# Attention and mixture of experts on one core: the 128-token slots move inside the 512-token windows, and three of them become 64-token slots with stacked halves

## The chip, the cores and the metric

The kernel runs on one core of a Trainium2 chip. The metric is the device time of one execution in microseconds. A measurement of this kernel can tell about 1% from no change.

## The reference

```python
scores = scale * np.matmul(q, k.transpose(0, 1, 3, 2))      # B=8, H=8, S=576, D=64
scores = np.where(masks[None], scores, -1e9)               # local (32 back) or strided (every 32nd)
attn = exp(scores - max); attn = attn / (attn.sum(-1) + 1e-09)
x = np.matmul(attn, v)  ->  [N=4608, D=512]
logits = x @ w_gate                                         # 8 experts
expert_idx = np.argmax(logits, axis=1)
for e in range(E):
    mask = expert_idx == e
    h = np.maximum(x[mask] @ w1[e], 0.0)                    # w1: 512 x 1024
    out[mask] = gate_w[mask, None] * (h @ w2[e])            # w2: 1024 x 512
```

Everything is float32. With the inputs that the reference draws, the eight experts get 591, 497, 610, 490, 661, 437, 657 and 665 tokens.

## The kernel before

The kernel first computes the attention, batch by batch, writes the rows x to DRAM (`xd`) and works out on the chip which token goes to which expert. The experts' work is cut into *jobs*. A **window** (`window`) is one expert's first 512 tokens: four tiles of 128. Experts 0, 2, 4 and 6 have two of their four tiles done early, in small windows (kind "F") beside the second half of the attention, so in the last phase (kind "B") experts 1, 3, 5 and 7 have windows of four tiles and experts 0, 2, 4 and 6 windows of two. What an expert has beyond 512 tokens goes into **slots** (`slot`): eight slots of up to 128 tokens, always all eight; which expert a slot serves is known only on the chip (`sids`, `souts` and `srow`, made by `e_slots1` to `e_slots4` on VectorE). What eight slots can't hold would go into a loop of dynamic slots at the end (`dynamic_slot`).

Every job streams its expert's weights in four chunks of 1 MB (`Chunk`): a DMA on SP's queue into `raw`, then ScalarE rounds it to `whi` (line 407) and VectorE makes the rest `wlo` (line 411), each in two halves of 128x1024. A product of float32 matrices is three TensorE products (high by high, high by low, low by high). Per chunk a slot does: 12 products of 256 columns (lines 602 to 604), a ReLU out of PSUM (`hr`, line 609 or VectorE), two 128x128 transposes (line 616), a split into `shh` (ScalarE) and `shl` (VectorE), and six products of 512 columns (lines 630 to 632). So each chunk of a slot passes from TensorE to ScalarE, back to TensorE, to ScalarE, to VectorE and back. A window's products are lines 530 to 532 and 503 to 505.

The order of the instructions on every engine is fixed when the program is built: a planner (`Line`) keeps a model of engines, buffers and eight PSUM banks, and again and again issues the operation that can start first, or of those near the first the one with the lowest `prio`, a due time. The costs and due times are written by hand. Each engine then runs its list in order on the chip. The jobs of the last phase have these due times, one after the other, each with a span of its own:

```python
jobs = [("w", 0)]
for e in range(1, E - 1):
    jobs += [("w", e), ("s", e - 1)]
jobs += [("s", s) for s in range(E - 2, RSLOT)] + [("w", E - 1)]
```

All weight chunks, of windows and slots, are chained (`chain_cp`): a chunk's rounding on ScalarE comes after that of the chunk that was added before it.

Of the kernel before, what the change touches and what calls it, by code (L numbers as in the profile page):

```python
# [36 lines left out]
RSLOT = 8  # L37
MAXSLOT = 40
# [13 lines left out]
AHEAD = 12000.0  # L52
F_LOAD = 92500.0
# [246 lines left out]
def moe_attn(ctx, tc, lqk, vl, sqk, vs, wg, wcat, blob, out):  # L300
# [50 lines left out]
    spacer = const.tile([128, 1], F32, name="spacer")  # L351

# [30 lines left out]
    chain_cp = [None]  # L383

    class Chunk:


        def __init__(self, prio, span, kind, load, deps=()):
# [11 lines left out]
            for h in range(2):  # L400
# [13 lines left out]
                hi = add(ACT, act_ns(1024), e_hi, [self.ld, chain_cp[0]], get=[self.hl] if h == 0 else [], put=[raw] if h else [],  # L414
                         prio=prio + 0.1 * span * h, kind=kind)
                lo = add(DVE, dve_ns(1024), e_lo, [hi], put=[raw], prio=prio + 0.1 * span * h, kind=kind)
                chain_cp[0] = hi
                self.parts.append((hi, lo))

    def gather_op(tag, pool, idc, rows, prio, kind, deps, cell):  # L420
        g = Slot(tag)

        def e_gather(_):
            cell["xg"] = buf(pool(), [128, XW], F32, "xg", g)
# [6 lines left out]
    def finish_ops(cell, yb, fin_deps, odc, slot_g, slots_y, ytag, ypool, prio, kind):  # L431
# [3 lines left out]
        def e_fin(e):  # L435
            y = buf(ypool(), [128, DM], F32, "y", yo)
            cell["y"] = y
# [5 lines left out]
        f = add(EITHER, eng, e_fin, fin_deps, get=[yo], put=[*slots_y, slot_g], prio=prio, kind=kind)  # L443
# [8 lines left out]
    def window(e, ranks, start, span, kind, deps, odeps, small, rows=N + 1, final=False):  # L452

        nt = len(ranks)

# [13 lines left out]
        for dc in range(4):  # L469
# [11 lines left out]
            def e_sp(e, dc=dc):  # L481
# [3 lines left out]
                     prio=start - AHEAD + 5.0 * dc, kind=kind, ins=2 * nt)  # L485
            h = add(ACT, act_ns(n), e_sp, [tr], put=[v, vn], prio=start - AHEAD + 5.0 * dc + 1, kind=kind)
            lo = add(DVE, dve_ns(n), e_sp, [h], put=[v, vn], prio=start - AHEAD + 5.0 * dc + 1, kind=kind)
# [68 lines left out]
    def slot(s, start, span, deps):  # L556

        kind = "B"

        def at(u):  # L560
            return start + span * u
# [3 lines left out]
        ga, g = gather_op("xg", lambda: moe["xgm"], lambda: sids[:, s:s + 1], N + 1, at(-0.8), kind, deps, cell)  # L565
# [3 lines left out]
        def e_tr(_):  # L569
            K["xh"] = buf(moe["slp"], [128, 4, 128], F32R, "sxh", sx)  # L570
            K["xl"] = buf(moe["slp"], [128, 4, 128], F32R, "sxl", sx)
            K["tb"] = bank(v)
            for dc in range(4):
                nc.tensor.transpose(K["tb"][:, dc * 128:(dc + 1) * 128], cell["xg"][:, dc * 128:(dc + 1) * 128], ident)

        def e_sp(e):
            split_to(K["tb"], K["xh"].rearrange("p c k -> p (c k)"), K["xl"].rearrange("p c k -> p (c k)"), e)

        tr = add(PE, 360, e_tr, [ga], get=[v, vn, sx], put=[g], prio=start - AHEAD, kind=kind, ins=8)
        h = add(ACT, act_ns(512), e_sp, [tr], put=[v, vn], prio=start - AHEAD + 1, kind=kind)  # L580
        lo = add(DVE, dve_ns(512), e_sp, [h], put=[v, vn], prio=start - AHEAD + 1, kind=kind)
# [7 lines left out]

        m2 = None  # L590
        for c in range(NCH):
            ch = Chunk(at(0.2 * c - 0.25), span, kind, lambda raw, c=c: load(c, raw), deps)
# [4 lines left out]
            def e_mm1(_, C=C, ch=ch, hb=hb):  # L597
                C["b"] = bank(hb)
                for dc in range(4):
                    w = slice(dc * CW, (dc + 1) * CW)  # L600
                    b = C["b"][:, 0:CW]
                    nc.tensor.matmul(b, K["xh"][:, dc, :], ch.hi[:, w], start=(dc == 0), stop=False)
                    nc.tensor.matmul(b, K["xh"][:, dc, :], ch.lo[:, w], start=False, stop=False)
                    nc.tensor.matmul(b, K["xl"][:, dc, :], ch.hi[:, w], start=False, stop=(dc == 3))

            def e_relu(e, C=C, hr=hr):
                C["r"] = buf(moe["slp"], [128, CW], F32, "hr", hr)
                if e == ACT:
# [4 lines left out]
            def e_ht(_, C=C, tv=tv):  # L613
                C["tb"] = bank(tv)
                for fl in range(2):
                    nc.tensor.transpose(C["tb"][:, fl * 128:(fl + 1) * 128], C["r"][:, fl * 128:(fl + 1) * 128], ident)

            def e_hs(e, C=C, sh=sh):
                if e == ACT:
                    C["h"] = buf(moe["slp"], [128, CW], F32R, "shh", sh)  # L620
                    C["l"] = buf(moe["slp"], [128, CW], F32R, "shl", sh)
                split_to(C["tb"][:, 0:CW], C["h"], C["l"], e)

            def e_mm2(_, C=C, ch=ch, c=c):
                if c == 0:
                    K["y"] = bank(yslot)
                for fl in range(2):
                    w = slice(1024 + fl * 512, 1024 + fl * 512 + 512)
                    ts = slice(fl * 128, (fl + 1) * 128)
                    nc.tensor.matmul(K["y"], C["h"][:, ts], ch.hi[:, w], start=(c == 0 and fl == 0), stop=False)  # L630
                    nc.tensor.matmul(K["y"], C["h"][:, ts], ch.lo[:, w], start=False, stop=False)
                    nc.tensor.matmul(K["y"], C["l"][:, ts], ch.hi[:, w], start=False, stop=(c == NCH - 1 and fl == 1))

            p = 0.2 * c
            m1 = add(PE, 12 * mm_ns(256), e_mm1, [*ch.parts[0], h, lo], get=[hb, hn], put=[sx], prio=at(p), kind=kind, ins=24)
            r = add(EITHER, both(256), e_relu, [m1], get=[hr], put=[hb, hn], prio=at(p + 0.001), kind=kind)
            ht = add(PE, 150, e_ht, [r], get=[tv, tn], put=[hr], prio=at(p + 0.002), kind=kind, ins=4)
            hh = add(ACT, act_ns(256), e_hs, [ht], get=[sh], put=[tv, tn], prio=at(p + 0.003), kind=kind)
            hl = add(DVE, dve_ns(256), e_hs, [hh], put=[tv, tn], prio=at(p + 0.004), kind=kind)
            m2 = add(PE, 6 * mm_ns(512), e_mm2, [hh, hl, *ch.parts[1]], get=[yslot, yhold] if c == 0 else [], put=[sh, ch.hl],  # L640
                     prio=at(p + 0.29), kind=kind, ins=12)
        return finish_ops(cell, lambda: K["y"], [m2], lambda: souts[:, s:s + 1], g, [yslot, yhold], "yo", lambda: moe["yp"], at(1.0), kind)
# [42 lines left out]
    def e_tiny(_):  # L685
# [529 lines left out]

    def prefix(src, name):
        for sh in (1, 2, 4):
            nx = pool().tile([128, E], F32, name=f"{name}{sh}")
            nc.vector.tensor_copy(out=nx[:, 0:sh], in_=src[:, 0:sh])
            nc.vector.tensor_tensor(out=nx[:, sh:E], in0=src[:, sh:E], in1=src[:, 0:E - sh], op=ALU.add)  # L1220
            src = nx
        return src

    def before(n, cum, weight, name):

        ge = wide(n, E)
        nc.vector.tensor_tensor(out=ge, in0=iota_sb[:, 0:n].unsqueeze(2).broadcast_to([128, n, E]),
                                in1=cum.unsqueeze(1).broadcast_to([128, n, E]), op=ALU.is_ge)
        es = pool().tile([128, n], F32, name=f"{name}_es")
        nc.vector.tensor_reduce(out=es, in_=ge, axis=AX.X, op=ALU.add)  # L1230
        nc.vector.tensor_tensor(out=ge, in0=ge, in1=weight.unsqueeze(1).broadcast_to([128, n, E]), op=ALU.mult)
        us = pool().tile([128, n], F32, name=f"{name}_us")
        nc.vector.tensor_reduce(out=us, in_=ge, axis=AX.X, op=ALU.add)
        nc.vector.tensor_tensor(out=us, in0=iota_sb[:, 0:n], in1=us, op=ALU.subtract)
# [11 lines left out]
    def e_slots1(_):  # L1246
        rem = pool().tile([128, E], F32, name="rem")
        nc.vector.tensor_scalar(out=rem, in0=cnt, scalar1=-float(BASE), scalar2=0.0, op0=ALU.add, op1=ALU.max)
        it128 = pool().tile([128, 32], F32, name="it128")
        nc.vector.tensor_scalar(out=it128, in0=iota_sb[:, 0:32], scalar1=128.0, scalar2=None, op0=ALU.mult)  # L1250
        cmp = wide(E, 32)
        nc.vector.tensor_tensor(out=cmp, in0=rem.unsqueeze(2).broadcast_to([128, E, 32]),
                                in1=it128.unsqueeze(1).broadcast_to([128, E, 32]), op=ALU.is_gt)
        sl["all"] = pool().tile([128, E], F32, name="rte")
        nc.vector.tensor_reduce(out=sl["all"], in_=cmp, axis=AX.X, op=ALU.add)
        sl["near"] = pool().tile([128, E], F32, name="near")
        nc.vector.tensor_scalar(out=sl["near"], in0=sl["all"], scalar1=float(NEAR), scalar2=None, op0=ALU.min)

    def e_slots2(_):
        sl["cum"] = prefix(sl["near"], "cumn")  # L1260

    def e_slots3(_):
        sl["es"], sl["us"] = before(RSLOT, sl["cum"], sl["near"], "st")

    def e_slots4(_):
        es, us = sl["es"], sl["us"]
        key = pool().tile([128, RSLOT], F32, name="skey")
        nc.vector.scalar_tensor_tensor(out=key, in0=us, scalar=float(E), in1=es, op0=ALU.mult, op1=ALU.add)
        no = pool().tile([128, RSLOT], F32, name="sno")
        nc.vector.tensor_scalar(out=no, in0=es, scalar1=float(E), scalar2=1000.0, op0=ALU.is_equal, op1=ALU.mult)  # L1270
        nc.vector.tensor_tensor(out=key, in0=key, in1=no, op=ALU.add)
# [5 lines left out]
        sf = pool().tile([128, RSLOT], F32, name="sf")  # L1277
        nc.vector.tensor_reduce(out=sf, in_=sel, axis=AX.X, op=ALU.add)
        nc.vector.tensor_copy(out=sids, in_=sf)
        out_index(souts, sf)  # L1280
        weight_row(srow, es)

    def e_slots5(_):
        had = sl["had"] = pool().tile([128, E], F32, name="had")
# [258 lines left out]
```

## Time and profile before

| | us |
|---|---|
| median of three runs | 669.93 |
| lowest, highest | 667.33, 671.51 |
| the profiled execution, its own time | 669.38 |
| its span, first to last instruction | 667.5 |

The profile is one execution. Its engines are PE (TensorE products), PEld (TensorE weight loads), DVE (VectorE), ACT (ScalarE), POOL (GpSimd) and SP (the queue of the weight DMAs). Products on PE overlap in a pipeline, so the duration of one is longer than the step from one to the next; the step is read from the starts in the timeline. "x" is a count; "<-" behind an idle time names what ended it.

### The profile page before, as it was taken

Reading aid. Unit: us, or ns where it says so; the run is one execution under the profiler, and the core shown is the slowest. Engines: PE = TensorE matmul, PEld = TensorE weight load, DVE = VectorE, ACT = ScalarE, POOL = GpSimd, SP = SyncE. Lnnn points to the kernel's source line nnn. Section 1 sums busy time; section 2 is a strip of 40 time slices with the busy share of each in tenths; the row PEclk is TensorE's granted clock in tenths of the full one; section 3 lists DMA queues with packets and bytes.
Section 4 is the critical chain, followed back from the end, with each engine's and each line's share of the span. In section 5 each row is a group of like instructions: output and inputs, shape, how many; then the busy total and the mean of one; then the engine's idle time right before and its main releaser. Section 6 shows DMA issues by size and latency. Waiting matters only on the chain. (4 is left out here: it accounts for less than half of the span.)

```text
span 667.5 us, 14798 instructions
## 1 busy us (share of the span) xinstructions
PE 628.3 (94%) x5927; PEld 523.2 (78%) x5928; DVE 410.7 (62%) x808; ACT 383.8 (57%) x736; POOL 180.7 (27%) x263
## 2 busy tenths in 40 slices
PE   4999989999999989999989999989999989998996
PEld 3777766887878778988878988878978878987884
DVE  3979887658776788862428672437672447688410
ACT  3687857575667575552356662366663366688311
POOL 3557545223516043120051220051210051110002
PEclk9999998999999999999999999999999999999999
DMA  8688859865554399653177673268682358596001
GB/s 336 228 294 299 271 183 402 318 227 203 181 193 168 108 395 384 240 178 139 64 251 289 212 291 148 87 229 297 213 324 102 108 200 324 206 314 247 4 0 66
DMA packets 30937, 145.58 MB, mean 218 GB/s; under 512 B 4750, under 2 KB 4878, under 8 KB 20625
## 3 DMA queue, kind: packets, MB, share of 16 engines
q1 hardware_dynamic: 23616, 123.78, 51.0%
q0 software_dynamic: 6432, 20.26, 8.4%
q8 instruction: 48, 0.79, 0.5%
q10 hardware_dynamic: 816, 0.56, 0.3%
q14 instruction: 25, 0.20, 0.1%
HBM read 125.41 MB, written 20.22 MB: 218 GB/s over the span
## 5 line engine op out<-in xcount | busy, mean ns | idle before, releaser
L411 DVE TENSOR_TENSOR wlo<-raw,whi 128x1024 fp32r<-128x1024 f32 x160 | 192.2, 1229 | 70.1 <-ACT whi L407 67.4
L407 ACT CAST whi<-raw 128x1024 fp32r<-128x1024 f32 x160 | 164.7, 1054 | 54.0 <-PE b L505 41.0
L530 PE MATMUL b<-xh,whi 128*128 128x256 f32 (+1 forms) x384 | 125.7, 327 | 0.5 <-issue 0.5
L532 PE MATMUL b<-xh,wlo 128*128 128x256 f32 (+1 forms) x384 | 123.3, 321 | 1.3 <-DVE wlo L411 1.1
L531 PE MATMUL b<-xl,whi 128*128 128x256 f32 (+1 forms) x384 | 122.7, 320 | 0.5 <-DVE xl L375 0.4
L540 ACT ACTIVATE hh<-b 128x256 fp32r<-128x256 f32 (+1 forms) x96 | 43.7, 455 | 122.0 <-PE b L532 118.4
L503 PE MATMUL b<-whi,hh 128*128 128x512 f32 x256 | 103.3, 404 | 2.0 <-ACT whi L407 1.4
L505 PE MATMUL b<-whi,hl 128*128 128x512 f32 x256 | 101.0, 395 | 1.4 <-DVE hl L543 1.4
L543 DVE SCALAR_TENSOR_TENSOR hl<-b,hh 128x256 fp32r<-128x256 f32 (+1 forms) x96 | 48.2, 507 | 86.4 <-ACT hh L540 86.2
L504 PE MATMUL b<-wlo,hh 128*128 128x512 f32 x256 | 100.9, 394 | 0.0
L530 PEld LDWEIGHTS b<-xh,whi 128*128 128x128 f32 x384 | 72.4, 189 | 9.0 <-issue 0.6
L532 PEld LDWEIGHTS b<-xh,wlo 128*128 128x128 f32 x384 | 72.4, 188 | 8.6 <-DVE wlo L411 3.0
L531 PEld LDWEIGHTS b<-xl,whi 128*128 128x128 f32 x384 | 72.5, 189 | 7.8 <-DVE xl L375 0.9
L425 POOL DMA_INDIRECT xg<-xd,ids x24 | 24.8, 1032 | 195.7 <-ACT y L439 163.6
L505 PEld LDWEIGHTS b<-whi,hl 128*128 128x128 f32 x256 | 48.0, 188 | 13.8 <-DVE hl L543 2.9
L503 PEld LDWEIGHTS b<-whi,hh 128*128 128x128 f32 x256 | 48.1, 188 | 10.5 <-ACT whi L407 1.6
L504 PEld LDWEIGHTS b<-wlo,hh 128*128 128x128 f32 x256 | 48.2, 188 | 8.0
L815 DVE TENSOR_REDUCE nm<-b 128x4 f32<-128x384 f32 (+2 forms) x64 | 32.9, 522 | 20.5 <-PE b L795 15.8
L446 POOL DMA_INDIRECT out_dram<-y,oids x24 | 27.8, 1158 | 63.2 <-ACT y L439 58.5
L375 DVE TENSOR_TENSOR xl<-b,xh 128x256 fp32r<-128x256 f32 (+1 forms) x48 | 23.4, 508 | 31.4 <-ACT xh L373 29.4
L848 POOL TENSOR_TENSOR probl<-probl,ri 128x384 f32<-128x384 f32 (+1 forms) x40 | 30.2, 762 | 43.4 <-DVE ri L844 32.3
L320 ACT COPY pT<-b 96x512 f32<-96x512 f32 (+3 forms) x62 | 33.6, 558 | 11.4 <-PE b L857 10.3
(176 smaller groups left out, 1099.7 us busy)
## 6 DMA issues: line engine op xcount, KB each, us to landing
raw<-in_wcat_dram SPq DMA_DIRECT2D x80, 1024.0 KB, 4.9
xd<-xr SPq DMA_DIRECT2D x36, 264.0 KB, 4.2
lqk_sb<-in_lqk_dram SPq DMA_DIRECT2D x16, 592.0 KB, 6.4
sqk_sb<-in_sqk_dram SPq DMA_DIRECT2D x16, 576.0 KB, 6.4
vst<-in_vs_dram SPq DMA_DIRECT2D x8, 704.0 KB, 9.1
vt<-in_vl_dram SPq DMA_DIRECT2D x8, 640.0 KB
xg<-xd,ids POOLq DMA_INDIRECT x24
out_dram<-y,oids POOLq DMA_INDIRECT x24
```

Source lines behind the costliest of these rows:

```text
L320: nc.scalar.copy(out=out, in_=in_)
L407: nc.scalar.copy(out=self.hi[:, sl], in_=self.raw[:, sl])
L411: nc.vector.tensor_tensor(out=self.lo[:, sl], in0=self.raw[:, sl], in1=self.hi[:, sl].bitcast(F32), op=ALU.subtract)
L503: nc.tensor.matmul(Y[t], H["h"][:, ts], ch.hi[:, w], start=(j == 0), stop=False)
L504: nc.tensor.matmul(Y[t], H["h"][:, ts], ch.lo[:, w], start=False, stop=False)
L505: nc.tensor.matmul(Y[t], H["l"][:, ts], ch.hi[:, w], start=False, stop=(j == 7))
L530: nc.tensor.matmul(b, ch.hi[:, w], X["h"][:, dc, :], start=(dc == 0), stop=False)
L531: nc.tensor.matmul(b, ch.hi[:, w], X["l"][:, dc, :], start=False, stop=False)
L532: nc.tensor.matmul(b, ch.lo[:, w], X["h"][:, dc, :], start=False, stop=(dc == 3))
L540: nc.scalar.activation(out=H["h"][:, 0:n], in_=H["b"][:, 0:n], func=AF.Relu)
L543: nc.vector.scalar_tensor_tensor(out=H["l"][:, 0:n], in0=H["b"][:, 0:n], scalar=0.0, in1=H["h"][:, 0:n].bitcast(F32), op0=ALU.max, op1=ALU ...
L815: nc.vector.tensor_reduce(out=nm[:, 0:nb], in_=sb[k][:, 0:w].rearrange("p (n k) -> p n k", k=step)[:, :, 0:win], axis=AX.X, op=ALU.max)
```

## The change

- A window's due times now hold its slots as well: `WITH` lists which slots run inside which expert's window. A window's span grows by 11 us for each full slot and 8 us for each short one, and the slots' due times are spread over it. Windows 1, 3 and 5 (four tiles) hold slots 0; 1 and 6; 2 and 3. Windows 2, 4 and 6 (two tiles) hold slots 5; 7; 4. Windows 0 and 7 hold none.
- The slots' weight chunks are chained among themselves, apart from those of the windows.
- Slots 5, 6 and 7 are short: up to 64 tokens. Their high and low halves lie side by side in one stationary operand, so that two products take the place of three; the two halves of the result lie in partitions 0 to 63 and 64 to 127. After the first layer a float32 product with `twice` (two 64x64 identities, one above the other) transposes and adds them, in place of the transpose; after the second layer ScalarE copies one half and VectorE adds the other, and ScalarE scales the sum.
- `e_slots1` to `e_slots5` sort the extra pieces into those over 64 tokens (slots 0 to 4) and those of up to 64 (slots 5 to 7), with more small VectorE instructions.
- Windows of the last phase have the transposes of their x due 18 us ahead in place of 12.

```diff
+RFULL = 5
+WITH = ((), (0,), (5,), (1, 6), (7,), (2, 3), (4,), ())
+SPLIT = 4000.0
+LATER = 3500.0
+STRETCH = 0.85
+FIRST_AT = 0.05
+AHEAD_W = 18000.0
...
-    chain_cp = [None]
+    chain_cp = {}
...
-                hi = add(ACT, act_ns(1024), e_hi, [self.ld, chain_cp[0]], ...
+                hi = add(ACT, act_ns(1024), e_hi, [self.ld, chain_cp.get(chain)], ...
...
+        def e_other(_):
+            cell["y"] = buf(ypool(), [128, DM], F32, "y", yo)[0:n]
+            nc.scalar.copy(out=cell["y"], in_=yb()[n:2 * n])
+        def e_sum(_):
+            nc.vector.tensor_tensor(out=cell["y"], in0=yb()[0:n], in1=cell["y"], op=ALU.add)
+        if n < 128:
+            f = add(ACT, 560, e_other, fin_deps, get=[yo], prio=prio, kind=kind)
+            f = add(DVE, 650, e_sum, [f], put=slots_y, prio=prio, kind=kind)
+            f = add(ACT, 600, e_fin, [f], put=[slot_g], prio=prio, kind=kind)
...
-    def slot(s, start, span, deps):
+    def slot(s, start, step, deps):
+        short = s >= RFULL
+        n = 64 if short else 128
...
+            if short:
+                K["h"], K["l"] = K["xh"][:, :, 0:n], K["xh"][:, :, n:2 * n]
...
+        def products(out, high, low, ch, w, first, last):
+            nc.tensor.matmul(out, high, ch.hi[:, w], start=first, stop=False)
+            nc.tensor.matmul(out, high, ch.lo[:, w], start=False, stop=short and last)
+            if not short:
+                nc.tensor.matmul(out, low, ch.hi[:, w], start=False, stop=last)
...
-            ch = Chunk(at(0.2 * c - 0.25), span, kind, lambda raw, c=c: load(c, raw), deps)
+            p = start + step * c
+            ch = Chunk(p - SPLIT, 12000.0, kind, lambda raw, c=c: load(c, raw), deps, "s")
...
+                    if short:
+                        nc.tensor.matmul(C["tb"][:, fl * n:(fl + 1) * n], C["r"][:, fl * 128:(fl + 1) * 128], twice, start=True, stop=True)
+                    else:
+                        nc.tensor.transpose(C["tb"][:, fl * n:(fl + 1) * n], C["r"][:, fl * 128:(fl + 1) * 128], ident)
...
+                if e == ACT:
+                    nc.scalar.activation(out=x[:, :, 0:n], in_=t, func=AF.Relu)
+                else:
+                    nc.vector.scalar_tensor_tensor(out=x[:, :, n:2 * n], in0=t, scalar=0.0, in1=x[:, :, 0:n].bitcast(F32),
+                                                   op0=ALU.max, op1=ALU.subtract)
...
+            ht = add(PE, 150, e_ht, [r, doubled], get=[tv, tn], put=[hr], prio=p + 20, kind=kind, ins=4)
...
+    def e_twice(_):
+        nc.gpsimd.tensor_tensor(out=twice, in0=ident[:, 0:64], in1=ident[:, 64:128], op=ALU.add)
...
+        for e in range(E):
+            tr = range(2 if e in EXP else 0, 4)
+            span = 11000.0 * len(tr) + sum(8000.0 if x >= RFULL else 11000.0 for x in WITH[e])
+            for n, x in enumerate(WITH[e]):
+                scattered = slot(x, start + span * (n + FIRST_AT) / len(WITH[e]), span * STRETCH / len(WITH[e]) / NCH, [sized, *allrows])
+            window(e, [(lambda t=t, e=e: ids[:, t, e:e + 1], lambda t=t, e=e: oids[:, t, e:e + 1]) for t in tr],
+                   start, span, "B", [made, *allrows], [mout], False, final=e == E - 1)
+            start += span
```

## Rows read from the trace of the kernel before

**Rows 1.** The page, busy time of each engine over the whole span, and TensorE's clock.

```profile
PE 628.3 (94%) x5927; PEld 523.2 (78%) x5928; DVE 410.7 (62%) x808; ACT 383.8 (57%) x736; POOL 180.7 (27%) x263
PEclk9999998999999999999999999999999999999999
```

**Rows 2.** Busy time by stretch, last phase: stretch, its length, each engine, clock, DMA.

```profile
214.00:338.00 124.00, 119.57 (x784) 101.12 (x783) 76.15 (x165) 62.85 (x103) 22.59 (x32) 1.00 0.57 213
338.00:360.00 22.00, 19.37 (x132) 17.02 (x131) 14.24 (x20) 15.13 (x28) 10.17 (x14) 1.00 0.68 239
...
436.00:460.00 24.00, 21.36 (x141) 18.64 (x140) 15.49 (x21) 15.99 (x28) 10.67 (x15) 1.00 0.67 225
...
536.00:558.00 22.00, 19.36 (x130) 16.97 (x130) 14.52 (x20) 15.13 (x27) 10.17 (x14) 1.00 0.65 228
558.00:600.00 42.00, 42.00 (x281) 37.90 (x280) 29.76 (x37) 29.95 (x49) 3.98 (x6) 1.00 0.81 282
600.00:616.00 16.00, 14.25 (x88) 11.94 (x88) 12.71 (x16) 12.43 (x22) 1.09 (x2) 1.00 0.71 254
```

**Rows 3.** Waits of PE from 338 to 616 us: total, times, longest.

```profile
PE b L630 <- ACT shh L373: 6.8, 6, 1.5
PE b L616 <- ACT hr L609: 1.6, 2, 0.8
```

**Rows 4.** Groups by line and shape, one line of each kind of product.

```profile
L602 PE MATMUL b<-whi,sxh 128*128 128x256 f32 x128 | 37.7, 295 | 0.0
...
L631 PE MATMUL b<-wlo,shh 128*128 128x512 f32 x64 | 25.3, 396 | 0.0
...
L999 PE MATMUL b<-xT,wg_sb 128*32 128x384 f32 x96 | 10.6, 495 | 0.0
```

**Rows 5.** Timeline of PE: start, duration. Products of 256 and 512 columns, and transposes.

```profile
358.23 0.28 PE L530 MATMUL b<-xh,whi 128*128 128x256 f32 x1
358.35 0.28 PE L531 MATMUL b<-xl,whi 128*128 128x256 f32 x1
...
359.05 0.39 PE L505 MATMUL b<-whi,hl 128*128 128x512 f32 x1
359.28 0.40 PE L503 MATMUL b<-whi,hh 128*128 128x512 f32 x1
```

**Rows 6.** Timeline of PE and ACT around one stall of a slot.

```profile
347.34 0.38 PE L616 MATMUL b<-cst,hr 128*128 128x128 f32 x2
348.76 0.37 ACT L373 CAST shh<-b 128x256 fp32r<-128x256 f32 x1 [2.75 <-PE b L616]
349.19 0.50 PE L630 MATMUL b<-whi,shh 128*128 128x512 f32 x1 [1.46 <-ACT shh L373]
```

**Rows 7.** Timeline of PE: transposes of a slot, and plain float32 products.

```profile
384.87 0.38 PE L616 MATMUL b<-cst,hr 128*128 128x128 f32 x2
...
385.33 0.40 PE L631 MATMUL b<-wlo,shh 128*128 128x512 f32 x1
...
221.78 1.15 PE L999 MATMUL b<-xT,wg_sb 128*32 128x384 f32 x12
...
112.05 0.29 PE L884 MATMUL b<-pT,vo 96*64 96x64 f32 x4
112.16 0.29 PE L884 MATMUL b<-pT,vt 96*64 96x64 f32 x4
```

**Rows 8.** Groups by line: the work on a weight chunk on DVE and ACT.

```profile
L411 DVE TENSOR_TENSOR wlo<-raw,whi 128x1024 fp32r<-128x1024 f32 x160 | 192.2, 1229 | 70.1 <-ACT whi L407 67.4 <-issue 2.4
L407 ACT CAST whi<-raw 128x1024 fp32r<-128x1024 f32 x160 | 164.7, 1054 | 54.0 <-PE b L505 41.0 <-DMA raw<-in_wcat_dram 8.2 <-PE b L632 4.4
```

**Rows 9.** The slots' sizes on DVE, and the row number that SP's queue waits for.

```profile
235.50 0.42 DVE L1252 TENSOR_TENSOR wide<-rem,it 128x256 f32<-128x256 f32 x1
...
260.88 0.17 DVE L1242 CAST srow<-st_es 128x8 int32<-128x8 f32 x1
...
L645 SPq TENSOR_LOAD <-srow x8: 267/276/519, 276.8 to 585.9; - x8
```

More of the change, by code (lines that the diff above doesn't have):

```diff
@@ L454, in window @@
         nt = len(ranks)
+        ahead = AHEAD if small else AHEAD_W
         def at(u):
@@ L635, in slot @@
[L635 to L639, printed above, removed]
@@ L640, in slot @@
-            m2 = add(PE, 6 * mm_ns(512), e_mm2, [hh, hl, *ch.parts[1]], get=[yslot, yhold] if c == 0 else [], put=[sh, ch.hl],
-                     prio=at(p + 0.29), kind=kind, ins=12)
-        return finish_ops(cell, lambda: K["y"], [m2], lambda: souts[:, s:s + 1], g, [yslot, yhold], "yo", lambda: moe["yp"], at(1.0), kind)
+                    products(K["y"], C["h"][:, ts], None if short else C["l"][:, ts], ch, slice(1024 + fl * 512, 1024 + fl * 512 + 512),
+                             c == 0 and fl == 0, c == NCH - 1 and fl == 1)
@@ L644, in row_load @@
+            m2 = add(PE, 2 * np_ * mm_ns(512), e_mm2, [hh, hl, *ch.parts[1]], get=[yslot, yhold] if c == 0 else [], put=[sh, ch.hl],
+                     prio=p + LATER, kind=kind, ins=4 * np_)
+        return finish_ops(cell, lambda: K["y"], [m2], lambda: souts[0:n, s:s + 1], g, [yslot, yhold], "yo", lambda: moe["yp"], p + LATER + 1000.0, kind, n)
     def row_load(in_tensor, engines):
@@ L1254, in e_slots1 @@
-        sl["all"] = pool().tile([128, E], F32, name="rte")
-        nc.vector.tensor_reduce(out=sl["all"], in_=cmp, axis=AX.X, op=ALU.add)
-        sl["near"] = pool().tile([128, E], F32, name="near")
-        nc.vector.tensor_scalar(out=sl["near"], in0=sl["all"], scalar1=float(NEAR), scalar2=None, op0=ALU.min)
-    def e_slots2(_):
-        sl["cum"] = prefix(sl["near"], "cumn")
+        cmp2 = row(E, "pieces")
+        sl["all"] = row(E, "rte")
+        for first, dst in ((64.0, cmp2), (0.0, sl["all"])):
+            nc.vector.tensor_scalar(out=steps, in0=iota_sb[:, 0:32], scalar1=128.0, scalar2=first, op0=ALU.mult, op1=ALU.add)
+            nc.vector.tensor_tensor(out=cmp, in0=rem.unsqueeze(2).broadcast_to([128, E, 32]),
+                                    in1=steps.unsqueeze(1).broadcast_to([128, E, 32]), op=ALU.is_gt)
+            nc.vector.tensor_reduce(out=dst, in_=cmp, axis=AX.X, op=ALU.add)
@@ L1262, in e_slots3 @@
     def e_slots3(_):
-        sl["es"], sl["us"] = before(RSLOT, sl["cum"], sl["near"], "st")
+        sl["es"], sl["us"] = before(sl["at"], sl["cum"], sl["wk"], "st")
     def e_slots4(_):
[L1266 to L1270, printed above, removed]
@@ L1276, in e_slots4 @@
                                 op=ALU.mult)
-        sf = pool().tile([128, RSLOT], F32, name="sf")
+        sf = row(RSLOT, "sf")
         nc.vector.tensor_reduce(out=sf, in_=sel, axis=AX.X, op=ALU.add)
@@ L1310, in moe_attn @@
         tiny = add(POOL, 1800, e_tiny, prio=first)
+        doubled = add(POOL, 250, e_twice, [more], prio=F_START + F_SPAN * len(EXP) - 20000, kind="B")
         zrow = add(POOL, 1500, e_zrow, prio=first + 1, dma=-2000)
@@ L1355, in moe_attn @@
         add(DVE, 3700, e_slots6, [far], prio=start + 200000, kind="B")
[L1356 to L1366 removed]
+        for e in range(E):
[5 more added lines that the diff above has]
+                   start, span, "B", [made, *allrows], [mout], False, final=e == E - 1)
+            if e == E - 1:
+                add(POOL, 6500, e_drain, [scattered], prio=start, kind="B")
```

190 lines of the change are left out of this document (111 added, 79 removed).

## The prediction

> **What bounds the kernel now.** I read the page first: PE, TensorE's products, is busy for 94% of the span its own weight loads beside them for 78%, and no other engine for two thirds of it, at the full clock in nearly every slice [rows 1]. So the time is the length of PE's list plus the holes in it, and what matters is where those holes are. A busy share can hide slack, since products overlap in the pipeline, so I read the step between starts in the timeline too: 0.12 us from one 256-column product to the next and 0.23 us for 512 columns [rows 5], back to back, for stretches of tens of microseconds. PE's list is really full there.
>
> Then the last phase by stretches. Everything up to about 214 us is the attention and the early windows, which are planned before the last phase opens and which the change leaves alone. From 214 to 662 us PE stands idle in few places: 124.00 - 119.57 = 4.4 us at the seam between the phases, then 2.63, 2.64, 2.64 and 1.75 us in the four stretches that hold slots beside windows of two tiles, 9.7 us together [rows 2]; between them almost nothing, and in 558 to 600, a two-tile window and slots mixed, nothing at all. The waits name what these four stretches wait for: a slot's second-layer products for ScalarE's `shh`, 6.8 us in six waits, and the transposes for `hr`, 1.6 us [rows 3]. One of them in the timeline: after the transposes at 347.34 the split on ScalarE and the way back last until 349.19, and for 1.46 us PE has nothing else in its list [rows 6]. It is latency, not a full engine: VectorE is busy for 14.24 of 22.00 us there.
>
> So two things can shorten the run: fewer products, and something else for PE to do while a slot's chunk is with ScalarE and VectorE. The change does both.
>
> **Products removed.** A slot issues 16 products of 256 columns from each of lines 602 to 604 (128 over eight slots) and 8 of 512 columns from each of lines 630 to 632 (64 over eight) [rows 4]. A short slot has two such lines in place of three. Three short slots drop 3 x 16 x 0.117 = 5.6 us and 3 x 8 x 0.232 = 5.6 us (0.117 and 0.232 are the steps of rows 5 to a third digit), together 11.2 us. They were on the engine that sets the end, so this counts in full unless another engine becomes late in the windows that get the short slots.
>
> **The product with `twice`.** In 12 chunks two transposes become two plain float32 products with 64 moving columns. The pair of transposes costs 0.23 us: from 384.87 to the start of line 631 at 385.33 lie the pair and one 512-column product of 0.23 [rows 7]. The trace has plain float32 products: the gating issues 48, and there are 96 records [rows 4], so each is two records. The nearest in columns are line 884's with 64: four records step 0.11 us [rows 7], two products side by side, so one product has 0.11 us and a pair 0.23, no more than now. The nearest in the stationary operand are the transposes, 0.11 us per record; a pair of products is four records, 0.45 us. So 0 to 0.22 us a chunk, 0 to 2.6 us in all; no gain, since the moving work is not smaller by either row. Neither row is nearer, so I take the middle, 1.3.
>
> The Trainium skill speaks against this edit: Perfetto Trace Analysis, section Transposes, says that a logical transpose should be done as a transpose and not as a standard matmul, and FP8 and Floating Point Precision, section TensorE Precision Notes, that true FP32 takes four passes. The trace agrees with four passes: twelve records of 384 columns of line 999, in three sets of four side by side, take about a microsecond [rows 7], some 0.33 us a set and twice that for a product, against 0.23 us for one high-low product of 512 columns. But it shows the transposes of 128 columns at 0.11 us too, as dear as a 256-column product. With transposes at a quarter of a plain product of the same columns, the pairs would cost 4 x 0.23 / 2 and the sum would be 2.8 us later instead of 1.3.
>
> **The slots' stalls.** The 9.7 us sit in the four stretches where slots stand alone or beside a two-tile window whose products are not ready. Spread over a window, each chunk has the window's products to cover its round trip (a window's half chunk is 12 first-layer products and 12 or 6 second-layer ones, 5.6 us or 2.8 us). In the four-tile windows VectorE is mostly free today. What could come back: windows 2 and 4 keep two tiles and now hold a short slot each. Such a window has 96 x 0.117 + 48 x 0.232 = 22.4 us of PE, some 24 with transposes, and the short slot 4 x (8 x 0.117 + 4 x 0.232) = 7.5, some 9 with transposes: 33 us. VectorE has 16 half chunks at 1.2 us [rows 8], about 19, and some 8 us of splits and sums: 27 of 33, about 82%. At 71% (29.76 of 42.00) PE lost nothing, at 79% (12.71 of 16.00) it lost 1.75 of 16.00, 11% [rows 2]. So the return is 0 to 0.11 x 66 = 7 us; I take 3, since a planner that knows both engines' costs runs the conversions ahead where buffers allow, as it does in 558 to 600. Net -6.7 us.
>
> **What moves, and its queues.** The slots' loads move on SP's queue in between the windows' loads, and there are still 80 MB of chunks. The first one waits for `srow`. It was made at 260.88 and SP read it from 276.8 on [rows 9], 16 us of slack, and window 1, in which slot 0 now stands, ends where the slots begin today, at 338 us, and is 192 products of 0.23 us long, so it begins at about 294; a load due some 8 us ahead of that still finds its number. The chain on VectorE before it grows: one more compare and reduce over 256 elements (0.42 us each [rows 9]) and some dozen small ones of about 0.17, about 3 us. What is queued behind them on VectorE there is `wlo` of windows 6 (early) and 0, and TensorE waits for that. That costs 0 to 3 us; VectorE is busy for 76.15 of the 124.00 us of that stretch and PE loses only 4.4 there [rows 2], so I take 0.5. The gathers on POOL move with their slots; POOL is busy for a tenth to a half of these stretches [rows 2]. The new wait of `ht` for `doubled` is for one add on POOL that is due far ahead; behind it on PE stands the whole list, but the add is long done. The finishing of a short slot (a copy, a sum, a scale) holds one bank for about 1 us longer and costs PE nothing while a bank is free. The second chain of roundings takes a rule away and costs nothing by itself. The earlier x transposes (18 us) hold a bank and `xh` earlier; `xh4` and `xh2` alternate, so they wait for no reader.
>
> **Sum**, against the profiled execution's own 669.4: -11.2 + 1.3 - 9.7 + 3 + 0.5 = -16.1, so 653. A measurement can tell about 1% (6.7 us) from no change, so this should show. The median of the runs is 0.6 above the profiled execution, which is less than I can claim. PE stays the bound at the end.
>
> **Rivals.** (1) *The stalls go with the slots.* A chunk of a slot still makes five hand-overs, the list is in order, and the windows' products may be planned just as tightly around it. Then the 9.7 us stay and only the products go: 669.4 - 11.2 + 1.3 + 0.5 = 660, or 663 with the 3 us. For it: the planner already could mix slots with the windows beside them, since it picks by readiness, and yet left these holes. Against: in 558 to 600 the mix has none.
>
> (2) *The conversions become the bound in windows 2 and 4.* Then two thirds of the 11.2 us (slots 5 and 7) buy nothing and the 7 us return: 669.4 - 3.7 + 1.3 - 9.7 + 7 + 0.5 = 665. For it: a short slot has the same weights to convert and a third fewer products. Against: four buffers let conversion run ahead into the four-tile windows, where VectorE has room.
>
> (3) *Slower: banks run out in the four-tile windows.* Four banks hold the window's sums and one the slot's, all window long; three are left for the window's first layer, the slot's first layer, and transposes, and the list is in order, so a late evacuation stops the window's products too. There are 20 slot chunks in windows 1, 3 and 5. If each makes PE wait as long as the longest wait of today, 1.46 us [rows 6]: 649.8 (the sum without returns) + 29 = 679. It decides from 18 waits of that size on (26 us, 676). Against: three banks are one for each of the three uses, and a window has 2.8 us of second-layer products while its bank is emptied. The Trainium skill, in Perfetto Trace Analysis, section Optimization Strategy, says that a gap that repeats on the engine that should be saturated can mean too little SBUF or PSUM for the next tile. The gap here does repeat (2.63, 2.64, 2.64), but the waits name a computation on its way and no bank.
>
> (4) *The change does not do what it says.* The split fits only if no more than five pieces are over 64 tokens and no more than three are up to 64. The reference's counts leave 79, 98, 128 + 21, 128 + 17 and 128 + 25 beyond 512: five and three, exactly. If one piece fell into the dynamic loop, its four chunks in series, each a load and four conversions (2 x 1.05 and at least 1.2 us [rows 8]) and its products, would add some 30 us: 685 or so.
>
> **How the numbers follow.** Forecast 653, chance 0.70 (its own range 645 to 660: all returns at zero and the 4.4 us at the seam partly gone, to 7 us of returns with the dear `twice`). Rival 1: 0.15, two thirds of it faster by over 1% (below 663). Rival 2: 0.07, within 1%. Rivals 3 and 4: 0.06 and 0.02, slower. That makes faster 0.80, within 1% 0.12 and slower 0.08. The range 644 to 665 holds the forecast and rivals 1 and 2.
>
> **What would show it.** Right: the products of the third kind fall to five eighths in the slots (80 and 40), PE's last phase has no repeated hole of 2.6 us, and its end comes about 16 us earlier with the same last window. The `twice` records show their step at once. Wrong: waits of PE for `hr`, `shh` or `shl` in windows 1 to 6 that sum to more than 10 us; for `wlo` in windows 2 and 4 (rival 2); for evacuations in windows 1, 3 and 5 (rival 3); any instruction of `dynamic_slot` (rival 4). The prediction also falls if the part before 214 us changes its length, which nothing in the diff asks for.

## The result, and the profile after

The changed kernel takes 661.71 us (median of 11 runs, 659.64 to 666.71) where the kernel before takes 669.11 beside it (median of 11, 663.67 to 673.34): a ratio of 0.990, interval 0.986 to 0.993. It is faster by 7.4 us, where 16 were predicted. The profiled execution took 661.96 us, its span is 660.2.

The waits of PE from 240 to 616 us come first, as they carried the prediction [rows 3]:

```profile
PE b L604 <- DMA xg<-xd,sids: 5.0, 1, 5.0
PE b L503 <- DMA xg<-xd,ids: 2.8, 2, 1.6
PE b L527 <- ACT hh L564: 1.8, 1, 1.8
PE b L529 <- DVE hl L567: 1.1, 1, 1.1
PE b L621 <- DVE sxh L383: 0.7, 1, 0.7
PE b L654 <- ACT hr L327: 0.6, 1, 0.6
```

The slots' waits for `shh` and `hr` are down from 8.4 us to 0.6. In their place stands something else: PE waits for gathered rows (`xg`), 5.0 us once for a slot's (`sids`) and 2.8 us in two waits for a window's (`ids`). Both kinds are followed by stretches of a lower granted clock, in the page's PEclk line, that were not there before [rows 1]; the busy share is as high as it was:

```profile
PE 620.8 (94%) x5880; PEld 519.7 (79%) x5880; DVE 416.2 (63%) x839; ACT 384.4 (58%) x737; POOL 186.9 (28%) x264
PEclk8999987999999999899999899999999999999999
```

The stretches, with the columns of rows 2:

```profile
214.00:338.00 124.00, 116.91 (x789) 100.24 (x789) 83.50 (x197) 64.70 (x108) 22.14 (x33) 0.99 0.62 226
338.00:360.00 22.00, 22.00 (x122) 18.86 (x121) 11.66 (x16) 13.34 (x22) 4.59 (x5) 1.00 0.38 128
360.00:372.00 12.00, 6.96 (x36) 5.83 (x36) 3.41 (x6) 2.78 (x6) 6.88 (x11) 0.86 0.90 304
436.00:460.00 24.00, 24.00 (x128) 20.20 (x126) 15.43 (x19) 14.07 (x24) 2.10 (x3) 1.00 0.66 235
536.00:558.00 22.00, 22.00 (x110) 18.17 (x110) 11.20 (x13) 11.27 (x17) 2.63 (x3) 1.00 0.52 188
...
600.00:616.00 16.00, 16.00 (x83) 13.53 (x82) 11.54 (x13) 10.86 (x15) 4.03 (x6) 1.00 0.13 51
...
264.60:267.90 3.30, 3.30 (x15) 3.08 (x13) 1.78 (x3) 1.60 (x2) 0.00 (x0) 0.50 0.16 20
...
367.00:370.30 3.30, 3.19 (x10) 2.59 (x11) 0.42 (x1) 0.37 (x1) 0.95 (x2) 0.50 0.96 375
```

The four stretches that lost 9.7 us now lose nothing, though they hold other work. The loss has moved: 5.0 of 12 us in 360 to 372, and 7.1 us in place of 4.4 at the seam between the phases (214 to 338). In the last two rows the granted clock is 0.50, 1.2 GHz, right after PE has stood idle for gathered rows.

Why a slot's rows come late is read in POOL's timeline (start, duration, and in brackets the idle time before and what ended it):

```profile
354.62 0.96 POOL L433 DMA_INDIRECT xg<-xd,ids  x1 [49.26 <-ACT y L449]
355.88 1.48 POOL L433 DMA_INDIRECT xg<-xd,ids  x1 [0.30 <-issue]
357.67 1.02 POOL L469 DMA_INDIRECT out_dram<-y,souts  x1 [0.31 <-issue]
...
358.99 1.15 POOL L433 DMA_INDIRECT xg<-xd,sids  x1 [0.18 <-issue]
```

POOL works through its list in order. The first gather shown is one of window 3's; it stood at the head of the queue for 49 us, until ACT's `y` had read one of the nine `xg` buffers. The gather of slot 5, which runs in window 2 and whose rows were needed first, lay behind it, with three instructions between them. It was issued at 358.99 and the rows were there at 367.11, 8 us later; the DMA engines are busy for 90% of 360 to 372. In the due times this is one number against another: a window's gathers are due 0.7 of its span ahead (`at(-0.7)`), and window 3's span has grown from 44 to 63 us, so its gathers are due 44 us ahead of it; a slot's are due 14 us ahead of the slot. PE at the same place:

```profile
367.11 0.69 PE L604 MATMUL b<-cst,xg 64*128 64x64 f32 x4 [5.04 <-DMA xg<-xd,sids]
...
368.32 0.63 PE L528 MATMUL b<-wlo,hh 128*128 128x512 f32 x1
368.75 0.63 PE L529 MATMUL b<-whi,hl 128*128 128x512 f32 x1
```

After the wait the step of a 512-column product is 368.75 - 368.32 = 0.43 us instead of 0.23. At the seam it is window 0's x transposes, now due 18 us ahead, that stand in PE's list at 261.35 and 263.30 before their rows are there. POOL's gathers and PE's transposes:

```profile
243.45 2.05 POOL L433 DMA_INDIRECT xg<-xd,ids  x1 [10.83 <-PE b L529]
...
252.56 0.99 POOL L433 DMA_INDIRECT xg<-xd,ids  x1 [0.19 <-issue]
253.85 0.96 POOL L433 DMA_INDIRECT xg<-xd,ids  x1 [0.30 <-issue]
```

```profile
261.35 0.33 PE L503 MATMUL b<-cst,xg 128*128 128x128 f32 x1 [1.21 <-DMA xg<-xd,ids]
263.30 0.55 PE L503 MATMUL b<-cst,xg 128*128 128x128 f32 x3 [1.62 <-DMA xg<-xd,ids]
```

The semaphores in the trace say which gather each of these waits for: those of 252.56 and 253.85. The four gathers before them, from 243.45 to 248.58, are window 1's, whose transposes start at 278.29. In the kernel before it was the other way round: window 0's gathers were the first two, at 241.36 and 242.68, and its transposes at 263.62 waited for nothing. The due times say why, as at slot 5: window 1 starts 22 us after window 0, and its span has grown from 44 to 55 us, so its gathers are due 38.5 us ahead of it, which is 16.5 us ahead of window 0's start, and window 0's own are due 15.4 us ahead.

The products went as predicted: the third kind is down from 128 and 64 [rows 4] to 80 and 40, and no instruction of `dynamic_slot` appears.

```profile
L624 PE MATMUL b<-whi,sxl 128*128 128x256 f32 x80 | 22.5, 282 | 0.0
L624 PE MATMUL b<-whi,shl 128*128 128x512 f32 x40 | 15.8, 394 | 0.0
```

And the product with `twice`, between two products of 512 columns:

```profile
393.84 0.55 PE L654 MATMUL b<-twice,hr 128*128 128x64 f32 x4
394.20 0.48 PE L527 MATMUL b<-whi,hh 128*128 128x512 f32 x1
394.52 0.39 PE L528 MATMUL b<-wlo,hh 128*128 128x512 f32 x1
```

A pair is four records. Counted as the prediction counted the pair of transposes, up to the second product behind it and less 0.23 for the first, it takes 394.52 - 393.84 - 0.23 = 0.45 us, against 0.23 for the transposes [rows 7].

### The profile page after: what moved, and what is told of

Same layout as the page of the kernel before. It is cut to its first block, busy times and chain, and to the rows that moved or that the text cites. A ratio compares the mean times of both kernels' runs of the same rounds, so it can differ in the third digit from the quotient of the medians.

```text
span 660.2 us, 14723 instructions
## 1 busy us (share of the span) xinstructions
PE 620.8 (94%) x5880; PEld 519.7 (79%) x5880; DVE 416.2 (63%) x839; ACT 384.4 (58%) x737; POOL 186.9 (28%) x264
## 5 line engine op out<-in xcount | busy, mean ns | idle before, releaser
L554 PE MATMUL b<-xh,whi 128*128 128x256 f32 (+1 forms) x384 | 127.1, 331 | 0.0
L527 PE MATMUL b<-whi,hh 128*128 128x512 f32 x256 | 106.2, 415 | 1.8 <-ACT hh L564 1.8
L433 POOL DMA_INDIRECT xg<-xd,ids x24 | 28.7, 1194 | 220.7 <-ACT y L449 205.6
L327 ACT COPY xT<-b 128x256 f32<-128x256 f32 (+3 forms) x86 | 31.6, 456 | 13.2 <-PE b L934 12.7
```

Of the source, the lines that this page charges most:

```text
L327: nc.scalar.copy(out=out, in_=in_)
L527: nc.tensor.matmul(Y[t], H["h"][:, ts], ch.hi[:, w], start=(j == 0), stop=False)
L554: nc.tensor.matmul(b, ch.hi[:, w], X["h"][:, dc, :], start=(dc == 0), stop=False)
```

## The theory after the result, and its rivals

Theory: the spreading removed the slots' stalls as forecast, but gathered rows now come late in two places, and each place costs its waits and a stretch at half clock behind them. Rivals: the short slots are worth less than 11.2 us; or the spreading itself is worth little, and the short slots alone would have done as much.

The runs came from chips on which the kernel before takes different times, 655 us in the first two sets and 669 us in the third; each ratio below is against the kernel before on the same chip. "Holes" is worked out from PE's timeline: from 225 us on, the step from each start to the next, less the usual step (0.23, 0.12 or 0.11 us), added up where over 0.35 us is left. "Half clock" is the time at 1.2 GHz from 225 us on, the run's last few us left out; half of it is lost at most. By the steps from start to start the loss beside the holes is 2.7 us in the first profile after, 5.7 in a0 and 2.3 in a1.

| run | us | ratio, interval | holes | half clock |
|---|---|---|---|---|
| before, first profile | 669.1 | | 16.5 | 0 |
| after, first profile | 661.7 | 0.990 (0.986 to 0.993) | 14.1 | 6.8 |
| e1, slots' gathers early | 649.1 | 0.991 (0.988 to 0.994) | 8.1 | 0 |
| e2, x transposes later | 645.5 | 0.983 (0.980 to 0.987) | 4.9 | 0 |
| e3, no short slots | 664.3 | 1.013 (1.010 to 1.016) | 12.8 | 10.2 |
| e4, short slots, old order | 654.2 | 0.997 (0.995 to 1.000) | 10.2 | 3.4 |
| b0, before again | 657.4 | 1.001 (0.999 to 1.004) | 8.3 | 0 |
| a0, after again | 658.0 | 1.003 (1.001 to 1.005) | 11.5 | 13.7 |
| e5, e1 and e2 together | 644.3 | 0.982 (0.979 to 0.985) | 4.7 | 0 |
| e6, e5 without short slots | 655.0 | 0.999 (0.996 to 1.001) | 6.1 | 0 |
| b1, before a third time | 669.3 | 1.001 (0.997 to 1.004) | 14.8 | 0 |
| a1, after a third time | 664.9 | 0.992 (0.989 to 0.995) | 15.8 | 6.8 |
| e7, e5 again | 656.1 | 0.980 (0.975 to 0.985) | 9.5 | 0 |

## Experiments

**e1: the slots' gathers due 36 us ahead in place of 14.**

```diff
-        ga, g = gather_op("xg", ..., start - AHEAD - 2000.0, kind, deps, cell, n)
+        ga, g = gather_op("xg", ..., start - AHEAD - 24000.0, kind, deps, cell, n)
```

> The changed kernel with one edit: a slot's gather is due 24 us instead of 2 us before its transposes, so that on POOL it stands ahead of the gathers of later windows. Theory (the gain was lost to a gather that came late): the 5.0 us wait of PE for slot 5's rows goes, and with it the half-clock spell that followed it (3.4 us at half the clock, 1.7 us lost), so about 655 us, 0.979 of the kernel before; TensorE is at the full clock from 270 us to the end. Rival (the windows with a short slot are bound by the conversions of weights, the gather's wait only hides that): the 5 us come back as waits for wlo in the same window, about 661 us.

Measured 649.1 us, ratio 0.991; the changed kernel as it is came to 1.003 on that chip (a0). Slot 5's gather now stands ahead of window 3's and is issued 49 us before PE needs the rows; POOL's timeline:

```profile
297.88 1.21 POOL L433 DMA_INDIRECT xg<-xd,sids  x1 [0.19 <-PE b L556]
348.41 0.97 POOL L433 DMA_INDIRECT xg<-xd,ids  x1 [49.31 <-ACT sxh L381]
```

No wait for `sids` is left and no stretch at half clock, though the two waits at the seam are still there, in PE's waits from 240 to 616 us:

```profile
PE b L503 <- DMA xg<-xd,ids: 2.5, 2, 1.8
```

So an earlier place in POOL's list takes that wait away.

**e2: the windows' x transposes due 12 us ahead, as before the change.**

```diff
-AHEAD_W = 18000.0
+AHEAD_W = 12000.0
```

> The changed kernel with one edit: the windows' x transposes are due 12 us ahead again, not 18. Theory: the two waits of PE for the rows of window 1 at the seam between the phases (2.8 us) and the half-clock spell behind them (3.4 us, 1.7 lost) go, the wait for slot 5's rows stays, so about 657 us, 0.983 of the kernel before. Rival (the seam is bound by the loads there, whatever is transposed first): the same idle time moves to the next product, about 661 us.

Measured 645.5 us, 0.983. Here the whole list of PE's waits from 240 to 616 us is

```profile
PE b L527 <- ACT hh L564: 1.6, 1, 1.6
PE b L654 <- ACT hr L327: 0.9, 1, 0.9
PE b L529 <- DVE hl L567: 0.9, 1, 0.9
```

Both waits for gathers are gone, the slot's too, although this edit names no slot. POOL's timeline:

```profile
350.40 0.96 POOL L433 DMA_INDIRECT xg<-xd,ids  x1 [48.40 <-ACT xh L381]
...
354.24 0.94 POOL L433 DMA_INDIRECT xg<-xd,sids  x1 [0.18 <-issue]
```

Slot 5's gather still stands behind window 3's, which is held for 48 us here too. But it is issued some 5 us ahead of the next burst of weights (DMA share 0.57 from 350 to 360 us, 0.93 from 360 to 372), and PE reads the rows at 358.33, 4.1 us after the issue, without a wait; in the changed kernel it was issued 1 us ahead of that burst and took 8.1 us. So the late place in the queue seems to decide only together with the DMA traffic that the gather then meets, and e2 escapes by a few us; no run varies the traffic alone. At the seam, too, the order on POOL is as in the changed kernel, window 0's gathers behind window 1's; PE asks for the rows later, at 265.66, and they are there. The gain of e2 is that of both waits, and it does not separate them. That the 6 us more of lead cost time on this chip, and bought none, is shown by e5 against e1, which differ in that edit alone: 644.3 and 649.1 us.

**e3: no short slots** (three products for all eight slots, everything else as in the change).

```diff
-        short = s >= RFULL
+        short = False
```

> The changed kernel with three full products in all eight slots (no stacked halves; slots 5 to 7 hold the same pieces of up to 64 tokens as 128 rows, the rest of them empty): the spreading alone. Theory (the products count in full, 11.2 us less about 1.9 us for the products with the doubled identity): 9 us later than the changed kernel, about 671 us, that is, the spreading alone gains nothing over the kernel before. Rival (in the two-tile windows the products were hidden behind the conversions): some 4 us later, about 666 us.

Measured 664.3 us, 1.013: the spreading by itself, with its gathers late, makes the kernel slower on this chip. It is 6.3 us above the changed kernel (a0), between the 9 of the theory and the 4 of the rival, so it does not decide between them. It waits for gathers like the changed kernel (4.5 and 3.3 us), so it says nothing on whether the spreading would pay with rows in time; e6 answers both.

**e4: short slots in the order of before**, the jobs one after the other, each slot with a span of 12 us. The due times inside a slot, its gather's (9.6 us ahead), the 12 us of the x transposes and the single chain of weights are those of before, too; the cut shows the order alone.

```diff
...
-            for n, x in enumerate(WITH[e]):
-                scattered = slot(x, start + span * (n + FIRST_AT) / len(WITH[e]), ...)
+            if job == "s":
+                scattered = slot(x, start, 2400.0, [sized, *allrows])
+                start += 12000.0
...
```

> Short slots alone: the job order, due times and the single chain of weights as in the kernel before, slots 5 to 7 with stacked halves. Theory: 669 minus 9.3 us, about 660 us, with the stalls of 2.6 us beside the slots still there. Rival (conversions bind the short slots): those slots now stand together behind window 6, four chunks of weights each in less TensorE time, so PE waits for wlo there and the time is 664 us or more.

Measured 654.2 us, 0.997 with an interval that ends at 1.000. The rival "short slots alone do as much" falls against e5 (644.3), but not against the changed kernel as it is, which takes 658.0 on this chip (a0). Three short slots in a row have too few products to cover their round trips; the waits of PE from 560 to 612 us are

```profile
PE b L654 <- ACT hr L327: 2.1, 2, 1.2
PE b L621 <- DVE shh L671: 1.7, 2, 0.9
```

Its due times were written by hand for the old order and were not tuned further, so this is the order with these due times, not the best that it could give.

**b0 and a0: both kernels again, unchanged, with profiles on the faster chip.**

> The kernel before, unedited, profiled and timed beside the next three on one chip: the first four experiments were timed beside runs of it with a median of 655.6 us, 13.5 below the 669.1 of the result, so the baseline moves by more than the effect. Theory (chips differ in the early phase, by the half-clock spells and the loads there): ratio 1.00, and from the seam on the same length as in the first profile, 434 us from the last transposes of the routing to the end. Rival (the stalls beside the slots are not always there): the last phase is some 10 us shorter than 434 and the waits for shh are missing.

> The changed kernel, unedited, beside the kernel before and the next two. Theory: ratio about 0.990 as in the result, the 5 us wait for slot 5's rows there again and a half-clock spell behind it. Rival (the first profile's wait was bad luck of one chip): the wait is missing and the ratio is 0.98 or less.

Measured 657.4 and 658.0 us, 1.001 and 1.003. The surprise is b0: with the same instructions in the same order the stalls that the prediction counted on are not there, and from the last transposes of the routing to the end it takes 424.8 us, not 434.0. The stretch of row 338 to 360, in which PE was busy for 19.37 us [rows 2]:

```profile
338.00:360.00 22.00, 21.05 (x136) 18.63 (x135) 14.68 (x20) 14.18 (x25) 7.31 (x10) 1.00 0.85 308
```

PE is idle for 1.6 us in this stretch, 436 to 460 and 536 to 558 together, where it was 7.9. So on this chip there was little for the spreading to remove, and the late gathers and the dearer transposes took all that the short slots gave.

**e5 and e6: both gather edits together, and the same without short slots.** e5 has the edits of e1 and e2, e6 that of e3 as well.

> Both edits of the first two experiments together: slot gathers due 24 us ahead of the transposes and x transposes of the windows due 12 us ahead. Theory: neither wait for rows is left, no half-clock spell between 240 us and the end, ratio to the changed kernel about 0.98, to the kernel before about 0.97. Rival (either edit alone had already removed both waits): the same as with either edit alone.

> As the kernel with both edits, but with three full products in all eight slots: the spreading alone with its gathers in time. Theory: 9 us more than the kernel with both edits (11.2 us of products, less 1.9 for the products with the doubled identity), and some 9 us less than the kernel before, since the stalls beside the slots are gone. Rival (conversions hide the products in the two-tile windows): 4 us more than the kernel with both edits.

Measured 644.3 us (0.982, faster than both kernels) and 655.0 (0.999). The pair gives the short slots with nothing in their way: 10.7 us. By the rows it should be 11.2, less 2.6 for `twice` (12 x 0.22), plus 1.4 of holes (6.1 against 4.7), so 10.0; the two profiles differ by 9.1 from the last transposes of the routing on. That is the theory's 9 and not the rival's 4. And e5 against a0 gives the price of the late gathers: 13.7 us by the medians, 12.2 by the profiles from that point on, of which 6.8 are holes (11.5 - 4.7) and 5.7 the clock. Of a0's three stretches at half clock one, at 248 us, stands behind a wait of 1.9 us for `hh` and not for rows; without the 1.6 us that it loses some 10.6 are left. On top of e2 the earlier slot gathers buy nothing that can be told (645.5 and 644.3). e6 against b0 leaves 0 to 2.4 us for spreading alone on this chip.

**b1, a1 and e7: before, after and e5 again**, on a chip where the kernel before takes 669 us, as in the first measurement.

> The kernel before once more, to see whether the stretches without matmuls beside slots, 2.6 us each at three places in its first profile (345 to 349 us and two like it) and none above 0.5 us in the second, belong to the kernel or to the circumstances of a profile. If they are the kernel's: products with gaps of 2.6 us again. If they belong to the chip it ran on: present where the kernel takes about 669 us, absent where it takes about 656 us. The ratio to itself is 1.000 within 0.004 either way.

> The changed kernel on the same chip. Theory (the stalls beside slots are what the change removes, and the late gathers are what it pays): 0.99 where the kernel before shows the stalls of 2.6 us, 1.00 where it shows none. Rival (the ratio is the same everywhere and the two earlier ratios, 0.990 and 1.003, differ by chance): 0.996 in both cases.

> The changed kernel with the slots' gathers 24 us ahead and the window's transposes 12 us ahead. Theory: 14 us under the changed kernel of the same chip, so 0.982 where the kernel before has no stalls of 2.6 us, 0.970 where it has them. Rival (the gathers' lateness belongs to a chip too): on a chip where the changed kernel shows no wait of TensorE for gathered rows, no gain over it.

Measured 669.3, 664.9 and 656.1 us: 1.001, 0.992 and 0.980. b1 has the stalls again, to the tenth as in the first profile (PE's waits from 320 to 600 us):

```profile
PE b L630 <- ACT shh L373: 6.8, 6, 1.5
```

So the ratio does differ between the chips, with the stalls. Where it does not do as the theory expected is e7: 8.8 us under a1, not 14. On this chip a1 has one stretch at half clock, 6.8 us at slot 5, against three of together 13.7 us in a0; so the clock returns 2.3 us and not 5.7, and the holes 6.3 (15.8 - 9.5): 8.6, about what was measured. e7 has more holes left than e5 (9.5 and 4.7); its waits from 225 to 660 us, where e5 has 1.6 for `hh`, 1.1 for `hl` and 1.0 for `hr`:

```profile
PE b L527 <- ACT hh L564: 2.0, 2, 1.7
PE b L654 <- ACT hr L327: 1.6, 2, 0.9
PE b L529 <- DVE wk L1339: 1.5, 1, 1.5
PE b L621 <- DVE shh L671: 1.1, 1, 1.1
...
```

The rival that the lateness of the gathers belongs to a chip falls: a1 waits 4.5 and 3.0 us for them, a0 4.0 and 2.4.

## Why the prediction was wrong

The step that failed is "What moves, and its queues", where it says that the gathers on POOL move with their slots, and costs that at nothing because POOL is busy for a tenth to a half; and the half sentence on the earlier x transposes, costed by bank and `xh` alone. A busy share says nothing of a queue that stands still at its head. Window 3's gather waited 49 us for a buffer with POOL idle meanwhile; slot 5's gather was behind that, and no term of the sum had a place for it. And the longer spans themselves reordered POOL's list: window 1's gathers went ahead of window 0's, and window 3's ahead of slot 5's.

Step by step, for the first two profiles, from the last transposes of the routing (233.57 us before, 234.81 after) to the end of the span: 434.0 and 425.4 us, a gain of 8.6.

- *Products, -11.2*: right. The counts are 80 and 40, and e6 against e5 shows it in time.
- *`twice`, +1.3*: 12 x (0.45 - 0.23) = 2.6 us, the upper bound of 0 to 2.6. The records step 0.11 us, as the transposes do; that half of rows 7 which stands side by side did not apply, and the middle between two rows, of which one was right, was wrong by 1.3. The dear case, 2.8, was nearer. The Trainium skill's rule that a transpose should not be done as a standard matmul (Perfetto Trace Analysis, section Transposes) has the direction right here: the trace agrees, with 0.45 us against 0.23 for the pair.
- *The slots' stalls, -9.7, and +3 returning*: right on the chip of the result. From 300 us on the holes fall from 12.3 to 2.0 us, slot 5's wait left out, so 10.3 are gone, net, against 6.7 forecast. (In holes the four stretches are 11.7 us and not 9.7: the end that the trace gives a product covers part of the hole behind it.) What returns is a wait for `hr` and `sxh` in passing, not for conversions: PE never waits for `wlo` in windows 2 and 4.
- *The seam, +0.5*: holes of 6.9 us in place of 4.2 up to 300 us, so 2.7. Of the 6.9, 3.2 are the two waits for window 0's rows (the expectation of e2 calls them window 1's), and 1.3 are the longer chain on VectorE: `hh` was there at 254.01, but `hl` came only behind the slots' sorting, and PE waited for it. The profiles of a1 and e7 name the chain's `wk` at this place, with 1.1 and 1.5 us.

```profile
256.96 0.17 DVE L1340 TENSOR_TENSOR wk<-wk,base 128x16 f32<-128x16 f32 x1
257.05 0.42 DVE L567 SCALAR_TENSOR_TENSOR hl<-b,hh 128x256 fp32r<-128x256 f32 x1
257.53 0.49 PE L529 MATMUL b<-whi,hl 128*128 128x512 f32 x1 [1.10 <-DVE hl L567]
```

- *Not in the sum*: slot 5's rows 5.2 us, and two stretches at half clock, 2.7 us.

Together -11.2 + 2.6 - 10.3 + 2.7 + 5.2 + 2.7 = -8.3, against -8.6 measured in that part. The spans differ by 1.2 us less, because the part before is longer by that; up to 233 us the programs differ in one add on POOL alone.

The rivals: the time is that of rival 1 (660 to 663), and its mechanism is wrong, for the stalls did not go with the slots. Rivals 2 to 4 did not occur. What the list of rivals lacked was a DMA that comes late because of what is queued ahead of it.

With the gathers in time, e7 stands 13.3 us below b1, against the 16.1 of the sum. So the sum was nearly one for the change with its gathers due in time; most of the rest is `twice`, 1.3 dearer than taken, and holes, of which 5.3 are gone (14.8 - 9.5) where 6.2 were forecast.

**What stays open.** Why the hand-overs from PE are slow on one chip and not on another. The place where it shows is the same pair of instructions: the first profile below is b1, the second b0. Line 604 is the last product of the half chunk, line 479 the x transposes, `xh` what ACT makes of them.

```profile
343.76 0.28 PE L604 MATMUL b<-whi,sxl 128*128 128x256 f32 x1
343.88 0.38 PE L479 MATMUL b<-cst,xg 128*128 128x128 f32 x2
343.93 0.38 ACT L609 ACTIVATE hr<-b 128x256 f32<-128x256 f32 x1 [1.02 <-PE b L604]
...
346.22 0.37 ACT L373 CAST xh<-b 128x256 fp32r<-128x256 f32 x1 [1.91 <-PE b L616]
```

```profile
338.13 0.40 ACT L609 ACTIVATE hr<-b 128x256 f32<-128x256 f32 x1
...
339.10 0.28 PE L604 MATMUL b<-whi,sxl 128*128 128x256 f32 x1
339.22 0.38 PE L479 MATMUL b<-cst,xg 128*128 128x128 f32 x2
...
339.64 0.37 ACT L373 CAST xh<-b 128x256 fp32r<-128x256 f32 x1 [1.11 <-PE b L479]
```

On the one chip `xh` starts 2.34 us after the start of the transposes that it reads, on the other 0.42; `hr` starts 0.17 us after the half chunk's last product, against 0.97 ahead of it. ACT is idle meanwhile. In b1 this happens in the same three places as in the first profile. Is it a late signal from PE, or late ends of the products themselves, which the trace only models? The semaphore events in the traces speak for the signal. In b0 PE's semaphore moves at 339.62 and 339.83 us, within 0.02 us of the modelled ends of the two pairs of transposes (lines 479 and 616); in b1 these end at 344.25 and 344.47, but the semaphore moves only at 346.19 and 346.24, when PE has started the next 12 products at the usual step. In the eight profiles of the faster chip no signal of PE from 225 us on comes more than 0.7 us behind its instruction, in the other five 12 to 19 of some 300 do. Those five also lack some semaphore events, so a part of the 12 to 19 can be gaps in the record; ACT's waits are not. Why a signal comes late is not shown. So the reading of rows 6, that the stalls are the latency of hand-overs, holds only for chips such as the one on which they were read. Open, too, is whether the old order on POOL alone would have spared the waits at the seam: no run has the new spans with window 0's gathers first.

## What to carry to other kernels

When work moves within a fixed order, follow each queue that it moves past, the idle ones above all: find what stands at the head of it, which buffer that waits for, and when the moved instruction is issued at the latest. Due times that are fractions of a span grow when the span grows, and fixed ones don't; a longer span can reorder a queue by that alone. And before a stall of a few us is counted as the kernel's, look at a second profile from another chip.

## What was not expected of the hardware

- The same program takes 656 us on one chip and 669 on another, at the full clock in the last phase on both. Of the 12 us, 6.6 are holes on PE (14.8 against 8.3); PE's idle time in the three stretches beside slots (338 to 360, 436 to 460, 536 to 558) is 7.9 on the slower chip and 1.6 on the other.
- A wait of PE of a few us can cost some 1 to 3 us more afterwards, through the clock. After slot 5's wait of 4.0 to 5.0 us the granted clock was 0.50 for 3.4 us (first profile) or 6.8 us (a0, a1). After waits of 1.2 and 1.6 us close together at the seam it fell in the first profile (264.6 us) and not in a1, which waited 1.5 us twice there; after a wait for `hh` of about 2 us at 248 us it fell in a0 (1.9 us) and not in a1 (2.0 us).
